# Attention chunks loaded in two row-interleaved transfers, and GpSimd's three products in another order

## The chip, the cores and the metric

The kernel runs on one core of one Trainium2 chip. The metric is the device time of one execution in microseconds, the lower the better. The engines are named as the profile names them: PE is TensorE (PEld its weight loads), DVE is VectorE, ACT is ScalarE, POOL is GpSimd, SP is SyncE, which here only issues DMAs (SPq).

## The reference

Two stages follow one another: a recurrent attention with a decaying state, and a mixture of experts on its output.

```python
B, H, S, D = 4, 8, 768, 48
for t in range(S):                          # per batch and head
    cur   = outer(u * k[t], v[t])
    y[t]  = r[t] @ (state + cur)
    state = w[t][:, None] * state + outer(k[t], v[t])
x = y.transpose(0, 2, 1, 3).reshape(B * S, H * D)     # 3072 tokens of 384
# each token with x @ w_skip > 0 goes to its best of 8 experts:
#   out = x + gate * (relu(x @ w1[e]) @ w2[e]);  other tokens keep x
```

## The kernel before

The attention works on 24 chunks (4 batches times 6 chunks of 128 steps) one after the other. Inside a chunk the recurrence is turned into matrix products. With q the product of the decays from a step to the end of the chunk, and rh the product from its start, the kernel forms three elementwise products, each of 128 x 512 words, all on POOL:

- kq = k times q (line 325 in `prep_keys`), which needs the first scan, q (DVE, line 308 in `prep_scan`);
- rk = r times k (line 317 in `bonus_keys`), which needs only the loaded chunk;
- rp = r times rh (line 334 in `prep_reads`), which needs the second scan, rh (DVE, line 330).

PE multiplies kq with rp into the scores (line 358), DVE masks them (line 364) and multiplies the bonus term (line 381), PE forms the outputs (lines 409 and 413), the state update (line 390), the transposes (line 348), the bonus sums from rk (line 377) and the turned rows (line 425). One pass of the loop over `s` does the outputs of chunk s, the scores of chunk s + 1 and the scans and products of chunk s + 2, so the rp of a chunk is read by PE one pass after it was made. The order of the work on every engine is the order in which it is written, since all of it stands under `tc.manual_schedule()`.

The chunk itself (r, k and w, 1545 words in each row, 128 rows; 96 rows for the two chunks at the ends of the array, which are the chunks 6 and 23 in order of work) is loaded by SP at line 172 into one of three buffers `wrk_sb`. A buffer comes free when the rp of the chunk that was in it is done, so SP waits for POOL before each load. Behind it in SP's queue stand, for each pass, two loads of the turned values vt (line 157), one of v (line 177), the store of an earlier chunk's output (line 435), and in nine passes a part of the expert weights (line 86). Chunks 0 to 4 are loaded in two column parts (`cuts`), the others in one piece. POOL also has the low halves of the weights to form in some passes (line 109) and one-hot rows for the router (line 538).

After the attention comes the mixture of experts, in which PE is busy all the time.

Of the kernel before, what the change touches and what calls it, by code (L numbers as in the profile page):

```python
# [43 lines left out]
V_OFF = K_OFF + NP * P  # L44
# [13 lines left out]
def rwkv_moe_kernel(ctx, tc, wrk, wrk0, vN, uP, wgs, wgp, w12, cst, out):  # L58
    nc = tc.nc
# [82 lines left out]
    with tc.tile_pool(name="att", bufs=2) as att, \  # L142
# [20 lines left out]
        cuts = {i: ((0, R_OFF), (R_OFF, V_OFF)) for i in range(5)}  # L163

        def load_chunk(i):
            b, c = seq[i]
            rows = wrk.rearrange("b c g d n -> (b c g d) n")
            at = 2 * D * chunk[i]
            t = wrk_sb[i % NBUF]
            to, at = (t, at - KO) if 0 < chunk[i] < n - 1 else (t[KO:LO], at)  # L170
            for c0, c1 in cuts.get(i, ((0, V_OFF),)):
                yield nc.sync.dma_start(to[:, c0:c1], rows[at:at + to.shape[0], c0:c1])

        def load_v(i):
            b, c = seq[i]
# [56 lines left out]
        def setup():  # L232
            nc.gpsimd.memset(u_sb, 0.0)
            for t in vt_sb[:3]:
                nc.gpsimd.memset(t, 0.0)
            drain(load_chunk(0))
            second, third = load_chunk(1), load_chunk(2)
            next(second)
            nc.sync.dma_start(c_sb[:, :C_IOTA], cst[:, :C_IOTA])
# [60 lines left out]
        def prep_scan(i):  # L300
            wk = work[i] = {}
            t = wrk_sb[i % NBUF]
            n_ = NP * CW
            a3 = lambda z: z.rearrange("p (a j) -> p a j", a=NP)
            wk["w"] = t
            wk["r"], wk["k"] = a3(t[:, R_OFF:K_OFF]), a3(t[:, K_OFF:V_OFF])
            q = wk["q"] = att.tile([P, NP, CW], F32, tag="q", name=f"q{i}", bufs=2)
            nc.vector.tensor_tensor_scan(  # L308
                q.rearrange("p a j -> p (a j)")[:, ::-1], t[:, 1:1 + n_][:, ::-1],
                ones_at[:, 1:1 + n_][:, ::-1], 0.0, op0=ALU.mult, op1=ALU.max)  # L310
            rk = wk["rk"] = att.tile([P, NP, P], F32, tag="rk", name=f"rk{i}")
            if i > 1:
                bonus_keys(i)

        def bonus_keys(i):
            t = wrk_sb[i % NBUF]
            nc.gpsimd.tensor_tensor(work[i]["rk"].rearrange("p a j -> p (a j)"),  # L317
                                    t[:, R_OFF:K_OFF], t[:, K_OFF:V_OFF], op=ALU.mult)

        def prep_keys(i):  # L320
            wk = work[i]
            heads = wk["w"][:, 0:NP * CW].rearrange("p (a j) -> p a j", a=NP)
            nc.vector.reciprocal(heads[:, :, 0:1], wk["q"][:, :, 0:1])
            kq = wk["kq"] = att.tile([P, NP, P], F32, tag="kq", name=f"kq{i}")
            nc.gpsimd.tensor_tensor(kq, wk["k"], wk["q"][:, :, 1:1 + P], op=ALU.mult)  # L325

        def prep_reads(i):
            wk = work[i]
            rh = wk["rh"] = att.tile([P, NP, CW], F32, tag="rh", name=f"rh{i}", bufs=2)
            nc.vector.tensor_tensor_scan(  # L330
                rh.rearrange("p a j -> p (a j)"), wk["w"][:, 0:NP * CW], reads_at[:, :NP * CW],
                rowsk, op0=ALU.mult, op1=ALU.max)
            rp = wk["rp"] = att.tile([P, NP, P], F32, tag="rp", name=f"rp{i}", bufs=3)
            nc.gpsimd.tensor_tensor(rp, wk["r"], rh[:, :, :P], op=ALU.mult)  # L334
            if i < 2:
                bonus_keys(i)
# [344 lines left out]
        with tc.manual_schedule():  # L681
# [3 lines left out]
            for s in range(-2, n + 1):  # L685
                on = lambda i: 0 <= i < n
                if s == -2:
# [4 lines left out]
                    for g in range(2):  # L692
                        at = 2 * (g ^ 1)
                        nc.sync.dma_start(wgp_sb[half(1), g, :, 2 * D:],
                                          wgp[half(g), at:at + 2, 2 * D:])
                if 3 <= s + 4 < n:
                    chunk_parts = load_chunk(s + 4)
                    if s + 4 in cuts:
                        next(chunk_parts)
                        load_v(s + 2)  # L700
                    drain(chunk_parts)
# [21 lines left out]
                if on(s + 2):  # L723
                    prep_scan(s + 2)
# [3 lines left out]
                if on(s + 2):  # L728
                    prep_keys(s + 2)
                    drip(pace[0])  # L730
                    prep_reads(s + 2)
# [387 lines left out]
```

## Time and profile before

| what | value |
|---|---|
| median of 3 runs | 279.83 us (278.13 to 283.46) |
| the profiled execution, its own time | 279.76 us |
| its span | 277.9 us |
| PE busy | 264.4 us (95%) |
| DVE busy | 211.9 us (76%) |
| ACT busy | 157.1 us (57%) |
| POOL busy | 146.6 us (53%) |
| chunk loads in one piece (128 rows) | 17, 772.5 KB each, 7.1 us from issue to landing in the median |

The shares are means over two unlike stages. The attention takes the first 130 us or so, the experts the rest; the change touches the first alone, so its views are read by stretch.

### The profile page before, as it was taken

The numbers are of one execution on the slowest core, as the hardware profiler recorded it, in microseconds if no ns is written. First come the engines' busy times: TensorE is split into PE (matmuls) and PEld (weight loads), VectorE is DVE, ScalarE is ACT, GpSimd is POOL, SyncE is SP. The second block draws the span as 40 slices with busy tenths as digits, with TensorE's granted clock in tenths as the row PEclk, the third lists the DMA queues.
The fourth block names the chain that finished last, engine by engine and source line by source line (L and its number), as shares of the span: only waits on it lengthen the run. The fifth ranks groups of instructions, "written<-read, shape, count | busy, mean of one in ns | idle before, by whom it ended". The sixth has DMA issues, their size and how long they took to land.

```text
span 277.9 us, 8937 instructions
## 1 busy us (share of the span) xinstructions
PE 264.4 (95%) x3599; PEld 244.0 (88%) x3600; DVE 211.9 (76%) x396; ACT 157.1 (57%) x456; POOL 146.6 (53%) x141
## 2 busy tenths in 40 slices
PE   8899799998999999899999999999999999999992
PEld 3688688887888888787999999999999999999992
DVE  7989789999999999972748597957859488594310
ACT  4365556775788857767326482926729276391300
POOL 6888677798999997984656636011030110201111
PEclk9999999999999999999999999999999999999998
DMA  7999999999877999961078997765662656700001
GB/s 244 279 300 326 322 331 366 374 333 312 270 229 253 319 351 344 267 233 61 28 227 302 337 310 255 240 229 225 225 248 81 235 212 226 266 14 28 9 5 42
DMA packets 26402, 64.33 MB, mean 231 GB/s; under 512 B 4062, under 2 KB 15380, under 8 KB 26352
## 3 DMA queue, kind: packets, MB, share of 16 engines
q1 hardware_dynamic: 24176, 58.37, 63.2%
q0 software_dynamic: 2048, 5.30, 6.0%
q8 instruction: 30, 0.49, 0.7%
q14 instruction: 20, 0.16, 0.2%
q10 hardware_dynamic: 128, 0.00, 0.0%
HBM read 56.61 MB, written 7.67 MB: 231 GB/s over the span
## 4 chain that ended last, share of the span: by engine, by line
PE 71%; DMA 8%; issue 6%; DVE 5%; POOL 4%; ACT 4%; SPq 0%; POOLq 0%; DVEq 0%
PE psO L927 7%; PE psO L929 7%; PE psO L928 6%; PE psH L901 6%; PE psH L902 6%; PE psH L903 6%; PE psY L409 6%; DMA wrk<-wrk 5%; PE psH L135 4%; PE psX L425 4%; PE psA L358 4%; PE psY L413 3%; PE psT L348 3%; PE psY L377 2%; DMA r<-w 2%
## 5 line engine op out<-in xcount | busy, mean ns | idle before, releaser
L838 POOL DMA_INDIRECT out<-fin,ids x16 | 16.9, 1054 | 95.2 <-DVE fin L936 89.2
L908 ACT ACTIVATE hh<-psH 128x240 fp32r<-128x240 f32 (+1 forms) x60 | 22.4, 374 | 54.4 <-PE psH L903 47.4
L901 PE MATMUL psH<-xTh,w1h 128*128 128x240 f32 x168 | 46.3, 276 | 0.0
L902 PE MATMUL psH<-xTl,w1h 128*128 128x240 f32 x168 | 46.3, 276 | 0.0
L903 PE MATMUL psH<-xTh,w1l 128*128 128x240 f32 x168 | 46.1, 274 | 0.0
L927 PE MATMUL psO<-w2h,hh 128*128 128x384 f32 (+1 forms) x120 | 40.9, 341 | 0.0
L929 PE MATMUL psO<-w2h,hl 128*128 128x384 f32 (+1 forms) x120 | 40.3, 335 | 0.0
L928 PE MATMUL psO<-w2l,hh 128*128 128x384 f32 (+1 forms) x120 | 40.2, 335 | 0.0
L364 DVE TENSOR_TENSOR asb<-psA,c_sb 128x512 f32<-128x512 f32 x48 | 30.6, 679 | 5.4 <-PE psA L358 5.3
L913 DVE SCALAR_TENSOR_TENSOR hl<-psH,hh 128x240 fp32r<-128x240 f32 (+1 forms) x60 | 24.2, 403 | 12.3 <-ACT hh L908 7.3
L317 POOL TENSOR_TENSOR rk<-wrk 128x512 f32<-128x512 f32 x24 | 30.7, 1278 | 4.2 <-DMA wrk<-wrk 1.6
L330 DVE TENSOR_TENSOR_SCAN rh<-wrk,rowsk,pss 128x520 f32<-128x520 f32 x24 | 31.1, 1297 | 2.3
L325 POOL TENSOR_TENSOR kq<-wrk,q 128x512 f32<-128x512 f32 x24 | 28.3, 1181 | 6.9 <-DVE q L308 4.9
L901 PEld LDWEIGHTS psH<-xTh,w1h 128*128 128x128 f32 x168 | 31.7, 189 | 0.1
L903 PEld LDWEIGHTS psH<-xTh,w1l 128*128 128x128 f32 x168 | 31.8, 189 | 0.0
L902 PEld LDWEIGHTS psH<-xTl,w1h 128*128 128x128 f32 x168 | 31.7, 189 | 0.0
L334 POOL TENSOR_TENSOR rp<-wrk,rh 128x512 f32<-128x512 f32 x24 | 28.4, 1182 | 5.4 <-DVE rh L330 4.1
L308 DVE TENSOR_TENSOR_SCAN q<-wrk,pss 128x520 f32<-128x520 f32 x24 | 29.5, 1229 | 0.6 <-ACT pss L595 0.4
L409 PE MATMUL psY<-asb,v 128*48 128x128 f32 x384 | 26.9, 275 | 2.6 <-DVE psY L381 2.5
L91 DVE TENSOR_TENSOR w2l<-r,w2h 128x512 fp32r<-128x512 f32 x42 | 27.8, 687 | 1.7 <-ACT w2h L90 1.6
L418 ACT COPY xT<-psY 128x512 f32<-128x512 f32 x24 | 14.1, 588 | 25.6 <-PE psY L413 20.6
L936 DVE SCALAR_TENSOR_TENSOR fin<-psO,gates,xg 128x384 f32<-128x384 f32 (+1 forms) x15 | 9.3, 618 | 25.0 <-PE psO L929 23.2
(159 smaller groups left out, 605.8 us busy)
## 6 DMA issues: line engine op xcount, KB each, us to landing
r<-w SPq DMA_DIRECT2D x48, 512.0 KB, 5.6
wrk<-wrk SPq DMA_DIRECT2D x17, 772.5 KB, 7.1
vt<-wrk SPq DMA_DIRECT2D x48, 96.0 KB, 5.8
v<-vN SPq DMA_DIRECT2D x24, 192.0 KB, 4.9
out<-x SPq DMA_DIRECT2D x24, 192.0 KB, 5.0
wrk<-wrk SPq DMA_DIRECT2D x5, 512.0 KB
wrk<-wrk SPq DMA_DIRECT2D x5, 260.5 KB
wrk<-wrk SPq DMA_DIRECT2D x2, 579.4 KB
```

What stands on the lines that cost most here:

```text
L308: nc.vector.tensor_tensor_scan(q.rearrange("p a j -> p (a j)")[:, ::-1], t[:, 1:1 + n_][:, ::-1], ones_at[:, 1:1 + n_][:, ::-1], 0.0, op0= ...
L317: nc.gpsimd.tensor_tensor(work[i]["rk"].rearrange("p a j -> p (a j)"), t[:, R_OFF:K_OFF], t[:, K_OFF:V_OFF], op=ALU.mult)
L330: nc.vector.tensor_tensor_scan(rh.rearrange("p a j -> p (a j)"), wk["w"][:, 0:NP * CW], reads_at[:, :NP * CW], rowsk, op0=ALU.mult, op1=AL ...
L334: nc.gpsimd.tensor_tensor(rp, wk["r"], rh[:, :, :P], op=ALU.mult)
L364: nc.vector.tensor_tensor(s, psa[g], tri.rearrange("p (o j) -> p o j", o=1).to_broadcast([P, NP, P]), op=ALU.mult)
L409: nc.tensor.matmul(y_at(a, g), v[:, 2 * a + g], wk["asb"][g][:, a], start=False, stop=True, skip_group_check=True)
L901: nc.tensor.matmul(ps, w1h[:, o:o + P], xTh[:, kc], start=(kc == 0), stop=False)
L902: nc.tensor.matmul(ps, w1h[:, o:o + P], xTl[:, kc], start=False, stop=False)
L903: nc.tensor.matmul(ps, w1l[:, o:o + P], xTh[:, kc], start=False, stop=(kc == KC - 1))
L927: nc.tensor.matmul(po, h[j, fc][0], w2h[:, o], start=(fc == 0), stop=False)
L928: nc.tensor.matmul(po, h[j, fc][0], w2l[:, o], start=False, stop=False)
L929: nc.tensor.matmul(po, h[j, fc][1], w2h[:, o], start=False, stop=(fc == FC - 1))
```

## The change

Chunks from 5 on, so far one DMA each, are loaded with two: the even rows and then the odd rows of the same tile, 64 rows each (48 for the two shorter chunks). The call of `bonus_keys` moves from the end of `prep_scan` to the end of `prep_keys`. From chunk 2 on, POOL then forms kq, rk, rp in place of rk, kq, rp.

```diff
-            for c0, c1 in cuts.get(i, ((0, V_OFF),)):
-                yield nc.sync.dma_start(to[:, c0:c1], rows[at:at + to.shape[0], c0:c1])
+            m = to.shape[0]
+            if i in cuts:
+                for c0, c1 in cuts[i]:
+                    yield nc.sync.dma_start(to[:, c0:c1], rows[at:at + m, c0:c1])
+            else:
+                for o in range(2):
+                    yield nc.sync.dma_start(to[o:m:2], rows[at + o:at + m:2, :V_OFF])
...
             rk = wk["rk"] = att.tile([P, NP, P], F32, tag="rk", name=f"rk{i}")
-            if i > 1:
-                bonus_keys(i)
...
             nc.gpsimd.tensor_tensor(kq, wk["k"], wk["q"][:, :, 1:1 + P], op=ALU.mult)
+            if i > 1:
+                bonus_keys(i)
```

On POOL, for chunks 5 and 6, before (the names carry the tile's number in the program; what stands in brackets are the counters that the instruction waits for, the DMAHW ones those of landed DMAs):

```order
L317 TENSOR_TENSOR rk_559<-wrk_90 128x512 [waits DMAHW4_49,PE_49,Pool_49]
L325 TENSOR_TENSOR kq_578<-wrk_90,q_557 128x512 [waits DVE_49,PE_49]
L334 TENSOR_TENSOR rp_582<-wrk_90,rh_580 128x512 [waits DVE_49]
L317 TENSOR_TENSOR rk_654<-wrk_88 128x512 [waits DMAHW2_49,PE_49,Pool_49]
L325 TENSOR_TENSOR kq_673<-wrk_88,q_652 128x512 [waits DVE_49,PE_49]
L334 TENSOR_TENSOR rp_677<-wrk_88,rh_675 128x512 [waits DVE_49]
```

And the same place after (lines 328, 320 and 339 are the old 325, 317 and 334):

```order
L328 TENSOR_TENSOR kq_580<-wrk_90,q_560 128x512 [waits DMAHW4_49,DMAHW5_49,DVE_49,PE_49]
L320 TENSOR_TENSOR rk_562<-wrk_90 128x512 [waits Pool_49]
L339 TENSOR_TENSOR rp_585<-wrk_90,rh_583 128x512 [waits DVE_49]
L328 TENSOR_TENSOR kq_676<-wrk_88,q_656 128x512 [waits DMAHW3_49,DMAHW4_49,DVE_49,PE_49]
L320 TENSOR_TENSOR rk_658<-wrk_88 128x512 [waits Pool_49]
L339 TENSOR_TENSOR rp_681<-wrk_88,rh_679 128x512 [waits DVE_49]
```

The product that needs no scan moved from ahead of the first scan's product to between the two that need scans, and the first product of a chunk waits for two landings.

On SP, from the load of chunk 6 on, before:

```order
L172 DMA wrk_88<-wrk 96x1545 [waits DMAHW2_49,Pool_49]
L157 DMA vt_92<-wrk 48x2x256 [waits DMAHW3_49]
L157 DMA vt_92<-wrk 48x2x256 [waits DMAHW4_49]
L177 DMA v_448<-vN 128x384 [waits DMAHW5_49,PE_49]
L435 DMA out<-x_451 128x384 [waits DMAHW6_49,Activation_49]
L172 DMA wrk_89<-wrk 128x1545 [waits DMAHW7_49,Pool_49]
L157 DMA vt_93<-wrk 48x2x256 [waits DMAHW0_49]
L157 DMA vt_93<-wrk 48x2x256 [waits DMAHW1_49]
L177 DMA v_543<-vN 128x384 [waits DMAHW2_49,PE_49]
```

And after (line 177 is now the chunk load, 182 the load of v, 440 the store):

```order
L177 DMA wrk_88<-wrk 48x1545 [waits DMAHW3_49,Pool_49]
L177 DMA wrk_88<-wrk 48x1545 [waits DMAHW4_49]
L157 DMA vt_92<-wrk 48x2x256 [waits DMAHW5_49]
L157 DMA vt_92<-wrk 48x2x256 [waits DMAHW6_49]
L182 DMA v_450<-vN 128x384 [waits DMAHW7_49,PE_49]
L440 DMA out<-x_453 128x384 [waits DMAHW0_49,Activation_49]
L177 DMA wrk_89<-wrk 64x1545 [waits DMAHW1_49,Pool_49]
L177 DMA wrk_89<-wrk 64x1545 [waits DMAHW2_49]
L157 DMA vt_93<-wrk 48x2x256 [waits DMAHW3_49]
```

Each pass has one DMA more. The eight landing counters are used in turn, so each DMA waits until the eighth one before it has landed: before, that made the load of v wait for the chunk load of the pass before (DMAHW2 above); after, it is the first load of vt that does (DMAHW3).

## Rows read from the trace of the kernel before

**Rows 1.** Busy time over the steady attention: engine busy us, instructions, PEclk, DMA share, GB/s
```profile
core 0: us, PE busy (x) PEld busy (x) DVE busy (x) ACT busy (x) POOL busy (x), PEclk, DMA share, GB/s
20.00:120.00 100.00, 94.95 (x2071) 83.20 (x2070) 93.04 (x144) 69.05 (x240) 87.07 (x81) 1.00 0.98 314
```
**Rows 2.** What PE waited for from 8 to 133 us: total us, times, longest
```profile
PE psY L409 <- DVE psY L381: 2.5, 5, 0.9
PE psY L377 <- issue: 1.6, 1, 1.6
PE psY L377 <- ACT xT L418: 1.1, 2, 0.9
```
**Rows 3.** Timeline of one pass with POOL idle: start us, us, engine, line
```profile
47.77 1.18 POOL L325 TENSOR_TENSOR kq<-wrk,q 128x512 f32<-128x512 f32 x1 [0.56 <-DVE q L308]
47.95 1.30 DVE L330 TENSOR_TENSOR_SCAN rh<-wrk,rowsk,pss 128x520 f32<-128x520 f32 x1
48.22 1.05 PE L358 MATMUL psA<-rp,kq 64*64 64x128 f32 x32
49.32 1.18 POOL L334 TENSOR_TENSOR rp<-wrk,rh 128x512 f32<-128x512 f32 x1 [0.38 <-PE psA L358]
50.46 1.29 POOL L317 TENSOR_TENSOR rk<-wrk 128x512 f32<-128x512 f32 x1
50.53 0.33 SPq L172 DMA_DIRECT2D wrk<-wrk  x1
53.09 1.05 PE L358 MATMUL psA<-rp,kq 64*64 64x128 f32 x32
```
**Rows 4.** Timeline of passes in which POOL is full, chunks 14 and 16
```profile
71.14 1.28 POOL L109 TENSOR_TENSOR w2l<-r,w2h 128x512 fp32r<-128x512 f32 x1
72.13 1.23 DVE L308 TENSOR_TENSOR_SCAN q<-wrk,pss 128x520 f32<-128x520 f32 x1
72.38 1.30 POOL L317 TENSOR_TENSOR rk<-wrk 128x512 f32<-128x512 f32 x1
73.63 1.19 POOL L325 TENSOR_TENSOR kq<-wrk,q 128x512 f32<-128x512 f32 x1
75.05 1.20 POOL L334 TENSOR_TENSOR rp<-wrk,rh 128x512 f32<-128x512 f32 x1
...
86.53 1.19 POOL L334 TENSOR_TENSOR rp<-wrk,rh 128x512 f32<-128x512 f32 x1
...
88.05 1.05 PE L358 MATMUL psA<-rp,kq 64*64 64x128 f32 x32
```
**Rows 5.** What SP's queue waited for: total us, times, longest
```profile
SPq L172 <- POOL rp L334: 21.2, 13, 3.1
...
SPq L157 <- DMA wrk<-wrk: 10.4, 7, 2.4
SPq L177 <- DMA wrk<-wrk: 10.1, 8, 2.0
```
**Rows 6.** The load of chunk 22 (issue, time to landing) and its first scan
```profile
101.00 0.33 SPq L172 DMA_DIRECT2D wrk<-wrk  x1
...
DMA to landing us min/median/max: 8.1/8.1/8.1
...
112.09 1.23 DVE L308 TENSOR_TENSOR_SCAN q<-wrk,pss 128x520 f32<-128x520 f32 x1
```
**Rows 7.** The first scan's own semaphore waits over the run: ns min/median/max
```profile
L308 DVEq EVENT_SEMAPHORE  x23: 21/136/1374, 3.4 to 116.0; - x23
```
**Rows 8.** The last chunk load, of 96 rows, and four stretches as in rows 1
```profile
106.64 0.34 SPq L172 DMA_DIRECT2D wrk<-wrk  x1
...
25.50:29.60 4.10, 3.55 (x95) 2.96 (x94) 3.82 (x6) 2.48 (x11) 3.35 (x3) 1.00 1.06 285
33.70:37.90 4.20, 3.75 (x86) 3.13 (x83) 3.30 (x5) 2.84 (x12) 3.07 (x3) 1.00 1.05 345
43.20:47.40 4.20, 4.20 (x94) 3.76 (x91) 4.09 (x6) 3.26 (x11) 3.60 (x3) 1.00 1.03 364
...
109.50:114.70 5.20, 4.80 (x105) 4.24 (x101) 4.99 (x11) 4.30 (x16) 4.84 (x5) 1.00 1.04 248
```

## The prediction

> **What bounds the kernel now.** [...] Four resources are nearly full, so the shares do not say which ends last. The list of what PE waited for does [rows 2]: in the whole stage it has six entries that sum to 6.3 us, the three largest are shown, and neither POOL nor a transfer is among the six (one of them, the 1.6 us, is a wait for nothing that the profile shows). PE and, close behind it, DVE set the pace. The timeline of a plain pass shows the pace as the distance between the scores of two chunks: 53.09 − 48.22 = 4.87 us [rows 3]. POOL and the transfers run beside this, and what counts of them is their margin.
>
> The margin of rp, the product that PE waits for: in the plain pass rp ends at 49.32 + 1.18 = 50.50 and its chunk's scores start at 53.09, so it has 2.6 us to spare [rows 3]. Where POOL also makes low halves and one-hot rows it runs without a pause and falls behind: the rp of chunk 16 ends at 86.53 + 1.19 = 87.72 and the scores start at 88.05, which leaves 0.33 us [rows 4].
>
> The margin of the chunk loads: SP issues a load as soon as rp frees the buffer (rp ends at 50.50, issue at 50.53 [rows 3]); SP is there first in 13 of them and waits 21.2 us in sum [rows 5]. The slowest load that the trace times is that of chunk 22: issued at 101.00, landed 8.1 us later at 109.1; its scan starts at 112.09, so 3.0 us are left [rows 6].
>
> **The change part by part.**
>
> *Order on POOL.* No product is added. In a plain pass kq starts when the first scan is done, before and after alike; POOL was idle there for 0.56 us, so rk did not hold it up [rows 3]. What changes is rp: it started at 49.32, when the second scan was done (47.95 + 1.30 = 49.25). After the change POOL goes from kq (47.77 + 1.18 = 48.95) to rk for 1.28 us and is free for rp at 50.2, so rp is some 0.8 us late by these rows (0.7 if successive products overlap by 0.05 us, as the starts of rp and rk, 1.14 us apart at 1.18 us each, show). PE's 2.6 us cover it: cost 0. The next load of the buffer is issued 0.8 us later too, and its 3.0 us cover that.
>
> In the full stretch the order would not matter if POOL never paused, but it will pause once: at chunk 14, POOL ended its extra work at 72.4 and did rk while the first scan ran (72.13 + 1.23 = 73.36) [rows 4]. After the change it must wait for that scan, and then does kq and rk (1.19 + 1.30) before rp, which starts at 75.9 instead of 75.05: 0.9 us late. POOL has no pause for the next passes, so the delay stays until it has one. At chunk 16 it meets a margin of 0.33 us, and PE starts the scores 0.9 − 0.33 = 0.55 us late. Once the pass has slipped by this, the later chunks have that much more margin. Cost 0.55 us, once; the bounds are 0 (if the small pauses ahead absorb it) and 0.9 us (if the next chunk has no margin at all).
>
> Does an earlier kq give something back? It can start at most one rk, 1.3 us, earlier in the full stretch. The transposes that read it stand behind the scores on PE, and those wait for rp. Gain 0.
>
> *One more wait.* Chunks 5 to 23 are 19 first scans that wait for two landings instead of one. The semaphore waits in front of this scan took at least 21 ns and 136 ns in the median [rows 7], most of it while DVE was still at work. 19 x 0.021 = 0.4 us is the cost if none is hidden, 0 if all is; a bound from the median is 2.6 us, but that contains true waiting. I take 0.2.
>
> *One more DMA on SP.* Issuing takes 0.33 us [rows 3], 19 times, in a queue that now waits 21 us for rp [rows 5]. Each DMA also waits for the eighth before it. That made the load of v wait for the chunk load of the pass before (10.1 us in 8 waits) [rows 5]; now the first vt load does, one DMA earlier in the queue, and v, the store and the weights stand behind it. They have a pass or more to spare. The next chunk load stands behind them too, but as a rule waits for rp even longer: cost 0.
>
> *Two half loads for one.* The bytes are the same, and so is the size of a row. Nothing can use the even rows alone, since the scan runs over all partitions at once: there is no gain from the first half's landing. The second issue is 0.4 us later than the first, and with rp's 0.8 us this makes 1.2 of the 3.0 us margin. If the halves move as fast as the whole, cost 0. If they do not, the price is in rows of this trace: two loads have 96 rows and not 128, and while they moved the queues were as full as ever, but carried less. The last, issued at 106.64, was under way in the stretch from 109.5 to 114.7: DMA share 1.04, but 248 GB/s; the other, of chunk 6, in that from 25.5 to 29.6: 1.06 and 285 GB/s. Like stretches with 128 rows moved 345 and 364 GB/s [rows 8]. So the way in which rows fall on the DMA engines matters here. In time: 5.2 us x (1 − 248/364) = 1.7 us lost with one load, and 4.1 us x (1 − 285/345) = 0.7 us with the other. No row shows 64 rows at a step of two at this size; the bounds are 0 and 1.7 us of DMA time for each load. I take a value near 0 for the forecast, because the halves are 64 and 64 rows, which 16 engines share as evenly as 128, where a 96-row tile begins at the 17th partition; the rest is the first rival.
>
> [...]
>
> *The sum.* 279.76 us of the profiled execution (277.9 of span and 1.9 around it; 0.07 below the median of the runs) + 0.55 (rp at chunk 16) + 0.2 (semaphores) + 0 (SP) + some 0.4 for a load that comes too late now and then where the weights share the queues = 280.9, so 281.
>
> **The rivals.**
>
> *The halves move slowly, and the DMA engines become the bound: slower.* For it: the rows of the 96-row loads, and that the engines have little room, 98% busy [rows 1]. Against it: what two halves cost is not in the trace. Price: 0.7 to 1.7 us for each of 19 loads, 13 to 32 us of DMA time. Room: the stage moves 31.4 MB in 100 us; at the 350 GB/s of the good stretches that is 90 us, so 10 us are free, and the landing margin gives 2 us more once. Left are 1 to 20 us: 281 to 300, and at the middle price of 1.2 us (23 us in sum) 11 us, 291. It decides from about 0.6 us for a load on (12 us in sum); 0.9 us a load (17 us) make 5 us and so pass 2%.
>
> *Eight landings in flight are too few.* Where the weights also stand in the queue (nine passes), SP's pass is two chunk issues (0.8), a wait of up to 2.4 us for the earlier load [rows 5] and four or five issues of 0.4: about 5.2 us against a pace of 4.87. The next load is then up to 0.35 us later in each of the nine passes, 3.2 us in sum, of which the margin covers 1.8. That gives 281 + 1.4, some 282, and shows as SP arriving after rp.
>
> *It is faster.* The ceiling is all of PE's waits in the stage, 6.3 us: 273.5. For it speaks only that POOL's first product could hold up something that the lists do not name; against it that PE's list does not name POOL at all.
>
> **How the numbers follow.** Forecast as summed, 281: 0.55. Slow halves: 0.33, of which 0.25 lie above 2%. Eight landings: 0.08. Faster: 0.04. Two per cent, 5.6 us, is about what a measurement of this kernel can tell from no change; its bounds are 274.2 and 285.4. Faster: 0.04. Slower: 0.25 from the halves and 0.05 from errors of the other two, 0.30. Within 2%: 0.66. For the range I go down to 278, the lowest run of before, and up to 292, just past the middle price of slow halves; above it lie some 0.12, below it 0.06.
>
> **What the profile after would show.** Right: in plain passes rp starts about 0.8 us later after the second scan, POOL has its pause ahead of kq, the scores still come 4.87 us apart; PE's list has one short wait for rp near 88 us; the chunk loads land with 1.5 us or more ahead of their scans; the stretch from 20 to 120 us moves the same 314 GB/s. Wrong: if DVE's first scan waits for wrk, or the GB/s fall at a DMA share of 1, the halves are slow; if SP issues chunk loads long after rp's end, the eight landings bind; if PE waits for rp in many passes, I have the margin of rp wrong.

## The result, and the profile after

The changed kernel takes 282.38 us (median of 6 runs, 281.13 to 285.49), the kernel before in the same comparison 280.15 us (6 runs, 278.13 to 283.46). The ratio is 1.010, with a 95% interval from 1.0058 to 1.0141: a small loss, of about 2.8 us by this ratio, inside the 2% band. Ratios, here and below, leave out on both sides the executions over 1.5% longer than the fastest of their kernel, so they differ a little from the ratio of the medians (here 1.008), and the traces of the 1 KB DMA and of the four buffers, which are of such executions, are left out. The profiled execution of the changed kernel took 281.13 us with a span of 279.3 us; that of the kernel before took 279.76 and 277.9.

The steady stretch, in the columns of [rows 1]:

```profile
20.00:120.00 100.00, 94.30 (x2037) 82.20 (x2040) 90.67 (x141) 67.71 (x234) 85.10 (x79) 1.00 0.95 306
```

All engines are a little less busy, the clock is the same, and the DMA engines fell from 0.98 to 0.95 and from 314 to 306 GB/s. They did not become full and slow; they stood idle more often.

What PE waited for from 8 to 133 us (total us, times, longest), the counterpart of [rows 2]:

```profile
PE psY L414 <- DVE psY L386: 4.2, 7, 1.7
...
PE psA L363 <- POOL rp L339: 0.6, 1, 0.6
```

PE now waits once for rp, 0.6 us. The other growth is behind DVE. What DVE's first scan waited for:

```profile
DVE q L313 <- DMA wrk<-wrk: 2.6, 2, 1.4
DVE q L313 <- ACT pss L600: 1.5, 1, 1.5
```

A chunk load came too late for the scan twice (at chunk 5 by 1.2 us, at chunk 11 by 1.4), which it did not in the trace of before, and once the scan waited 1.5 us for a copy on ACT (0.4 us before). What SP waited for, beside [rows 5]:

```profile
SPq L177 <- POOL rp L339: 8.8, 5, 2.6
SPq L157 <- DMA wrk<-wrk: 8.1, 12, 1.4
SPq L177 <- DMA wrk<-wrk: 4.2, 7, 0.8
SPq L182 <- DMA wrk<-wrk: 2.5, 3, 1.1
```

L177 is now the chunk load and L182 the load of v. SP was at the chunk load before rp freed the buffer 5 times, not 13, and the chunk load itself waited for landings 7 times. Its waits for landed chunk loads did not grow in sum: 8.1 + 4.2 + 2.5 = 14.8 us, where the two entries of [rows 5] make 20.5. What grew is the time that an issue takes. The issues of the chunk loads from 20 to 120 us, before and after (count, then shortest, median and longest in ns):

```profile
L172 SPq DMA_DIRECT2D wrk<-wrk x18: 327/328/390, 22.1 to 106.6; - x18
```
```profile
L177 SPq DMA_DIRECT2D wrk<-wrk x36: 472/480/1022, 23.3 to 111.6; - x36
```

Two halves take 2 x 0.48 us in the median where one load took 0.33, so 0.63 us more for each chunk and 11 us for the 18. SP's wait for rp shrank by about as much, from 21.2 to 8.8 us.

A plain pass, beside [rows 3]:

```profile
46.73 1.05 PE L363 MATMUL psA<-rp,kq 64*64 64x128 f32 x32
...
51.00 1.18 POOL L328 TENSOR_TENSOR kq<-wrk,q 128x512 f32<-128x512 f32 x1 [1.18 <-DVE q L313]
51.18 1.30 DVE L335 TENSOR_TENSOR_SCAN rh<-wrk,rowsk,pss 128x520 f32<-128x520 f32 x1
...
51.60 1.05 PE L363 MATMUL psA<-rp,kq 64*64 64x128 f32 x32
52.13 1.27 POOL L320 TENSOR_TENSOR rk<-wrk 128x512 f32<-128x512 f32 x1
53.36 1.18 POOL L339 TENSOR_TENSOR rp<-wrk,rh 128x512 f32<-128x512 f32 x1
```

The second scan ends at 51.18 + 1.30 = 52.48 and rp starts at 53.36, 0.88 us later, where it was 0.07 before. The scores come at 51.60 − 46.73 = 4.87 us, as before.

The full stretch, chunks 14 and 16, beside [rows 4]:

```profile
73.66 1.18 POOL L328 TENSOR_TENSOR kq<-wrk,q 128x512 f32<-128x512 f32 x1 [0.26 <-issue]
...
74.79 1.28 POOL L320 TENSOR_TENSOR rk<-wrk 128x512 f32<-128x512 f32 x1
76.03 0.21 POOL L587 TENSOR_TENSOR gds<-gall,vals 128x10 f32<-128x10 f32 x1
76.19 1.19 POOL L339 TENSOR_TENSOR rp<-wrk,rh 128x512 f32<-128x512 f32 x1
...
87.70 1.20 POOL L339 TENSOR_TENSOR rp<-wrk,rh 128x512 f32<-128x512 f32 x1
...
88.95 0.97 PE L363 MATMUL psA<-rp,kq 64*64 64x128 f32 x29 [0.55 <-POOL rp L339]
```

The rp of chunk 16 ends at 88.90 and the scores start at 88.95: the margin of 0.33 us is used up.

The load of chunk 11 (its buffer is freed by the rp in the first row; SP's rows are DMA issues):

```profile
44.10 1.20 POOL L339 TENSOR_TENSOR rp<-wrk,rh 128x512 f32<-128x512 f32 x1
44.21 0.94 SPq L157 DMA_DIRECT2D vt<-wrk  x2
...
45.25 1.09 SPq L182 DMA_DIRECT2D v<-vN  x1
...
46.44 0.38 SPq L440 DMA_DIRECT2D out<-x  x1
46.87 0.42 SPq L86 DMA_DIRECT2D r<-w  x1
...
47.38 1.21 SPq L177 DMA_DIRECT2D wrk<-wrk  x2
...
56.00 1.24 DVE L313 TENSOR_TENSOR_SCAN q<-wrk,pss 128x520 f32<-128x520 f32 x1 [1.40 <-DMA wrk<-wrk]
```

The buffer was free at 45.30, but SP came to the two halves at 47.38, 2.1 us late: it was still getting through the turned rows, v, the store and a weight load. The scan stood still for 1.40 us. In [rows 3] the issue follows the end of rp by 0.03 us. Before, the load of chunk 11 went out 2.22 us ahead of the scores of chunk 8 (48.22 in [rows 3]):

```profile
46.00 0.33 SPq L172 DMA_DIRECT2D wrk<-wrk  x1
```

After, its first half went out 0.65 us behind these scores (46.73), so 2.9 us later against the pace.

The end of the stage, chunk 23:

```profile
118.14 1.20 POOL L339 TENSOR_TENSOR rp<-wrk,rh 128x512 f32<-128x512 f32 x1
119.28 0.23 POOL L591 TENSOR_TENSOR vals<-gds,vals 128x8 bf16<-128x8 f32 x1
119.54 0.20 ACT L600 CAST pss<-vals 128x40 f32<-128x40 bf16 x1 [1.29 <-POOL vals L591]
119.77 1.24 DVE L313 TENSOR_TENSOR_SCAN q<-wrk,pss 128x520 f32<-128x520 f32 x1 [1.50 <-ACT pss L600]
```

A small product of the router (vals) stands behind rp on POOL; ACT copies it, and DVE's last first scan comes behind that copy. So a late rp makes this scan late, whether or not PE needs the rp.

**Where the time went.** The table gives, from the timelines, the start of a chunk's scores minus the start of the same chunk's scores in the kernel before, in us. A step between two columns is time lost there, by whatever cause. The kernels of the other rows are those of the experiments.

| kernel | chunk 9 | 13 | 15 | 16 | 22 | 23 |
|---|---|---|---|---|---|---|
| changed kernel | −1.49 | +0.17 | +0.17 | +0.90 | +0.89 | +1.58 |
| order alone | +1.18 | +1.95 | +1.95 | +2.68 | +2.66 | +3.34 |
| split alone | −1.07 | +1.99 | +1.37 | +1.37 | +1.36 | +1.36 |
| new order where POOL pauses | −1.13 | −1.05 | −1.05 | −0.65 | −0.66 | +0.02 |
| new order for chunks 2 to 13 | −0.26 | +0.12 | +0.13 | +0.52 | +0.51 | +0.50 |
| split with paired v | −1.68 | −1.24 | −1.24 | −1.24 | −1.23 | −1.23 |
| order kq, rp, rk | −1.93 | −0.31 | −0.21 | −0.13 | +0.76 | +1.48 |

The offset at chunk 9 is no part of the change: the profiled execution of before had the 1.6 us wait for nothing that the profile shows [rows 2], which some profiled executions have, of either order (2.1 us in the order alone), and others not. The late scan of chunk 5 lies ahead of chunk 9 as well, so what it cost is hidden in the offset. From there the changed kernel loses 1.66 us by chunk 13 (late loads), 0.73 at chunk 16 (rp) and 0.69 at chunk 23 (the router's product): 3.08 us in one execution, by the ratio 2.8.

### The profile page after: what moved, and what is told of

Same layout as the page of the kernel before. It is cut to its first block, busy times and chain, and to the rows that moved or that the text cites. A ratio compares the mean times of both kernels' runs of the same rounds, so it can differ in the third digit from the quotient of the medians.

```text
span 279.3 us, 8971 instructions
## 1 busy us (share of the span) xinstructions
PE 265.2 (95%) x3599; PEld 244.2 (87%) x3600; DVE 211.4 (76%) x396; ACT 157.4 (56%) x456; POOL 146.9 (53%) x141
## 3 DMA queue, kind: packets, MB, share of 16 engines
q1 hardware_dynamic: 24480, 58.37, 62.7%
## 4 chain that ended last, share of the span: by engine, by line
PE 48%; issue 4%; POOL 3%; ACT 1%; DVE 0%; POOLq 0%
PE psO L932 7%; PE psO L934 6%; PE psO L933 6%; PE psH L907 6%; PE psH L906 6%; PE psH L908 6%; PE psH L135 4%; PE psX L836 2%; PE psO L676 2%; PE psY L414 1%; POOL out L843 1%; POOL hot L543 1%; PE psY L418 1%; POOL rk L320 0%; ACT xT L423 0%
```

## The experiments

All ratios are to the kernel before, run on the same chip. Line numbers differ by a few from kernel to kernel.

### Each part alone

The order alone: rk issued behind kq, chunk loads in one piece.

```
-            if i > 1:
-                bonus_keys(i)          # behind the first scan
...
+            if i > 1:
+                bonus_keys(i)          # behind kq
```

> Only the order on POOL (kq, rk, rp); chunk loads in one piece. If the order costs what the trace after shows (PE waits 0.6 us for rp at chunk 16, and the last scan waits for the router's values that stand behind rp on POOL, 0.7 us more): 0.7 to 1.5 us, ratio 1.003 to 1.006, with one PE wait for rp near 88 us and no scan that waits for wrk. If the late loads were all of the cost: ratio within 0.001 of 1, and no PE wait for rp.

Measured: 280.75 us (12 runs), ratio 1.0059 [1.0017, 1.0101]. PE's and DVE's waits:

```profile
PE psA L358 <- POOL rp L334: 0.5, 1, 0.5
...
DVE q L308 <- ACT pss L595: 1.5, 1, 1.5
```

The same two losses as in the changed kernel, 0.73 at chunk 16 and 0.68 at chunk 23 in the table, and no first scan waits for a load. Together 1.4 us; the ratio is worth 1.6. The table's step of 0.77 us from chunk 9 to 13 is not put down to the order: most of it is a wait of PE of 0.6 us for nothing that the profile shows (line 348), and the kernel with paired v alone, in the old order, has the same wait.

The split alone: two loads of alternate rows from chunk 5 on, the old order.

```
+                for o in range(2):
+                    yield nc.sync.dma_start(to[o:m:2], rows[at + o:at + m:2, :V_OFF])
```

> Only the two row-interleaved loads; old order on POOL. If the eight landing counters are the cause (one DMA more in each pass): 0.5 to 1.7 us, ratio 1.002 to 1.006; SP comes to a chunk load after rp has ended in passes with weights, and one or two scans wait up to 1.5 us for wrk; the stretch 20 to 120 moves 305 to 315 GB/s. If slow rows were the cause: ratio above 1.01 and fewer GB/s at a DMA share of 1. If only the order costs: ratio within 0.001 of 1.

Measured: 280.73 us (12 runs), ratio 1.0064 [1.0028, 1.0100]. DVE's and SP's waits:

```profile
DVE q L313 <- DMA wrk<-wrk: 3.0, 3, 1.6
```
```profile
SPq L157 <- DMA wrk<-wrk: 8.6, 14, 1.3
SPq L177 <- POOL rp L339: 7.8, 5, 2.0
SPq L177 <- DMA wrk<-wrk: 5.4, 8, 1.5
```

PE waits nowhere for rp, the table shows no loss at chunks 16 and 23, and the late loads are there, at chunks 5, 11 and 12. So in these traces the two parts cost separate things, and 0.6% + 0.6% makes about the 1.0% of both, within the intervals.

This execution lost more by the late loads than the changed kernel did (2.44 us against 1.66), and TensorE's clock has a part in it. Behind the late scans of chunks 11 and 12 PE stood still for 2.35 us, and then the granted clock fell to 0.50 for some 3 us (its mean from 20 to 120 us is 0.98):

```profile
66.95 1.08 PE L414 MATMUL psY<-asb,v 128*48 128x128 f32 x16 [2.35 <-DVE psY L386]
...
68.64 1.70 PE L363 MATMUL psA<-rp,kq 64*64 64x128 f32 x29
```
```profile
69.00:70.00 1.00, 1.00 (x30) 1.00 (x27) 0.90 (x3) 0.52 (x1) 1.00 (x1) 0.50 1.07 432
```

The scores, 1.05 us in a plain pass, took over 1.70. The table's +1.99 at chunk 13 holds this; by chunk 15 0.62 us of it had come back, and how much of the 2.44 us is left of it no run isolates. In the trace of the changed kernel the longest such wait is 1.70 us, and the clock stayed at 1.00.

### Is it the way in which the rows fall?

Two halves of neighbouring rows (0 to 63, 64 to 127) in place of even and odd rows; and four interleaved loads of 32 rows. Both with the old order.

```
+                for o in range(2):
+                    ro = slice(o * m // 2, (o + 1) * m // 2)
+                    yield nc.sync.dma_start(to[ro], rows[at + ro.start:at + ro.stop, :V_OFF])
```
```
+                for o in range(4):
+                    yield nc.sync.dma_start(to[o:m:4], rows[at + o:at + m:4, :V_OFF])
```

> Old order on POOL; two loads of neighbouring rows, 0 to 63 and 64 to 127, in place of even and odd. Eight counters: the same as the even and odd rows, ratio 1.002 to 1.006. If it matters which rows one load writes: 64 neighbouring rows move more slowly than 64 at a step of two, the DMA engines are full at 250 to 290 GB/s, scans wait for wrk in many passes, ratio 1.02 to 1.06.

> Old order on POOL; each chunk from 5 on in four interleaved loads of 32 rows. Eight counters: a pass now has eight DMAs, nine with weights, so each waits for its own place in the pass before; a pass cannot be shorter than a load takes to land, 4.5 to 6 us: ratio 1.01 to 1.04, with SP's waits for landed DMAs several times those of two loads. If only the rows and not the number of DMAs mattered: as with two loads.

Measured: neighbouring halves 300.1 us (6 runs), ratio 1.0779 [1.0711, 1.0846]; four loads 289.22 us (6 runs), ratio 1.0409 [1.0339, 1.0480]. The steady stretch, first of the neighbouring halves, then of the four loads:

```profile
20.00:120.00 100.00, 86.94 (x1776) 75.64 (x1775) 80.21 (x121) 58.66 (x200) 74.39 (x66) 0.95 1.04 255
```
```profile
20.00:120.00 100.00, 89.66 (x1901) 78.68 (x1899) 85.78 (x131) 62.78 (x217) 79.03 (x71) 0.98 0.88 280
```

Both move fewer bytes a second, but in opposite ways: with neighbouring halves the DMA engines are full (1.04) at 255 GB/s; with four loads they are less busy (0.88). In both the first scans wait for late loads (7.6 and 5.5 us in sum), and the mean granted clock falls, to 0.95 and 0.98. The page's row of the main DMA queue (packets, MB, share of 16 engines' span) for before, the changed kernel, neighbouring halves and four loads:

```profile
q1 hardware_dynamic: 24176, 58.37, 63.2%
```
```profile
q1 hardware_dynamic: 24480, 58.37, 62.7%
```
```profile
q1 hardware_dynamic: 24480, 58.37, 68.6%
```
```profile
q1 hardware_dynamic: 25056, 58.37, 61.8%
```

Multiplied by the spans (277.9, 279.3, 297.8, 286.5 us) the same 58.37 MB take 175.6, 175.1, 204.3 and 177.1 us of the engines' time. Even and odd rows cost no time on the DMA engines; neighbouring halves cost 28.7 us, or 1.5 us for each of 19 loads. The rival of slow halves is false for this change and true for its neighbour. The four loads cost hardly any engine time either (1.5 us in all), yet 4%: with three more DMAs a pass the engines are not fed. SP's waits and its issues of chunk loads in that kernel:

```profile
SPq L157 <- DMA wrk<-wrk: 1.6, 1, 1.6
SPq L177 <- DMA wrk<-wrk: 1.5, 3, 0.8
```
```profile
L177 SPq DMA_DIRECT2D wrk<-wrk x70: 469/586/1597, 19.6 to 116.0; - x70
```

I had expected several times the waits of two loads (8.6 and 5.4), and they nearly vanish. Four issues of 0.59 us take 2.3 us of a pass of 4.87, and those of the other DMAs come on top. By these rows issuing fills the queue here, and not waits for landings.

Neighbouring halves and alternate rows are the same bytes in the same 24480 packets, and the first took 204.3 us of the engines' time, the second 175.1. What makes the difference no run here shows.

### Is it one DMA more?

The kernel before, with a DMA of 1 KB that nobody reads, behind each chunk load from 5 on; no half loads, old order.

```
+            if i not in cuts:
+                yield nc.sync.dma_start(extra[:, 16 * i:16 * i + 16], cst[:16, 16 * i:16 * i + 16])
```

> Old order, chunk loads in one piece, and behind each from chunk 5 on one DMA of 1 KB that nothing reads: the same number of DMAs in each pass as with two half loads, no row moved otherwise. If the eight landing counters are the cost of the split: as e2, ratio 1.003 to 1.009, with SP waiting for the chunk load of the pass before at the first vt load. If the halves themselves were the cost: ratio within 0.002 of 1.

Measured: 281.31 us (12 runs), ratio 1.0084 [1.0046, 1.0122]. A DMA more in SP's queue costs about as much as the split does, with no chunk load touched. It adds an issue and a landing both, so it does not tell these two apart.

Would a fourth buffer help, so that the loads could be issued a pass earlier? The split alone, with four buffers for the chunks:

```
-        wrk_sb = [pers.tile([P, V_OFF], F32, name=f"wrk{i}") for i in range(NBUF)]
+        NWRK = 4
+        wrk_sb = [pers.tile([P, V_OFF], F32, name=f"wrk{i}") for i in range(NWRK)]
```

> Old order, the two interleaved loads, and four chunk buffers in place of three, so that SP need not wait for the rp of the pass before. If late chunk loads are the cost of the split: they land a pass earlier, no scan waits for wrk, ratio 0.998 to 1.003. If the split costs elsewhere (more semaphores on DVE and POOL): as e2, 1.003 to 1.009.

Measured: 281.67 us (12 runs), ratio 1.0071 [1.0032, 1.0110]. It gives nothing back that can be told from the noise. That fits the waits of the split alone, where SP waits for rp only 5 times (7.8 us): where it comes behind rp anyway, a buffer that is free earlier changes nothing.

And would fewer DMAs? From chunk 6 on one load brings v of two chunks, the same bytes in nine DMAs fewer; once with the split, once without.

```
+            elif i % 2 == 0:
+                v2 = att.tile([P, 2, H, D], F32, tag="v2", name=f"v{i}", bufs=3)
+                nc.sync.dma_start(v2, vN[b, c:c + 2].rearrange("c p h d -> p c h d"))
+                v_sb[i], v_sb[i + 1] = v2[:, 0], v2[:, 1]
```

> The old order on GpSimd, two interleaved half loads as in the change, and from chunk 6 on one load brings v of two chunks: the same bytes, nine DMAs fewer from chunk 7 to 23. If the number of DMAs in flight is what the split costs (one more in each of 19 passes: 1.006), half of them are given back: 1.002 to 1.004 against the kernel before, and SP's waits for landings in the v and turned-row loads fall by about half. If the cost lies in the half loads themselves, it stays at 1.006.

> The kernel before with v of two chunks in one load from chunk 6 on; chunk loads in one piece, old order. If the number of DMAs in flight held anything up before the change, this is faster: 0.996 to 0.999. If the kernel before was never held up there (its first scans wait for no load), 0.998 to 1.002.

Measured: with the split 280.71 us (12 runs), ratio 1.0045 [1.0009, 1.0082]; without 279.56 us (12 runs), ratio 1.0002 [0.9973, 1.0031]. In the first one's trace the split's loss is mostly gone, 0.44 us from chunk 9 to 15 (split alone: 2.44). Its one scan that waits for a load is that of chunk 1, ahead of the split loads:

```profile
7.33 1.24 DVE L318 TENSOR_TENSOR_SCAN q<-wrk,pss 128x520 f32<-128x520 f32 x1 [1.02 <-DMA wrk<-wrk]
```

This execution took 279.23 us, though, 1.5 less than the kernel's median; the median's ratio, 1.0045, lies between the half that was expected and no gain at all, and the interval holds both. Without the split, fewer DMAs change nothing that can be measured.

### The order on GpSimd

The new order only where the trace of before shows pauses on POOL (chunks 2 to 13, 20 and 21); then for chunks 2 to 13 alone. Chunk loads in one piece.

```
-            if i > 1:
+            if i > 1 and i not in between:
                 bonus_keys(i)          # behind the first scan
...
+        between = set(range(2, 14)) | {20, 21}
...
+            if i in between:
+                bonus_keys(i)          # behind kq
```

> Chunk loads in one piece; kq, rk, rp only for the chunks 2 to 13, 20 and 21, where POOL has pauses; the old order for 14 to 19, 22 and 23. If the late rp at chunk 16 and the late router values at chunk 23 are the cost of the order: ratio 0.998 to 1.002, no PE wait for rp. If the plain passes cost something as well (later issue of the loads): 1.003 or more, with scans that wait for wrk.

> One-piece loads; the new order on GpSimd for chunks 2 to 13 only, the old one from 14 on. If the 0.68 us that the last scan waits longer comes from the new order in chunks 20 and 21, which leaves GpSimd later for its last router product, that wait is back at 0.4 us or less, the pass of chunk 23 loses nothing against the kernel before, and PE waits for rp nowhere: 0.996 to 1.002. If the loss at chunk 23 has another source, the scan still waits about 1.5 us.

Measured: 279.8 us (12 runs), ratio 1.0012 [0.9974, 1.0051]; and 281.19 us (12 runs), ratio 1.0035 [0.9994, 1.0076]. Neither is told apart from no change. The traces say more: the loss at chunk 16 is 0.40 and 0.39 us where it was 0.73, and that at chunk 23 is still 0.68 in the first and gone in the second, whose last scan is back to

```profile
DVE q L308 <- ACT pss L599: 0.3, 1, 0.3
```

So the new order in chunks 20 and 21 is what puts the router's product behind, as expected. My expectation that PE would wait for rp nowhere was wrong: it waits 0.2 us at chunk 16 in both (and 0.8 us at chunk 0 in the second, where the order is the old one). It looks as if POOL enters the full stretch later even when only the chunks ahead of it have the new order.

The other sign, scans that wait for a load, is there in both, at chunks 5 and 6 in the first and 6 and 12 in the second:

```profile
DVE q L308 <- DMA wrk<-wrk: 1.3, 2, 0.7
```
```profile
DVE q L308 <- DMA wrk<-wrk: 1.5, 2, 1.3
```

So late loads are not the split's alone. Whether the later rp brings these is open: the order alone has none, and paired v alone, in the old order, has one of 0.5 us.

The changed kernel with the old order for chunks 14 to 19, 22 and 23 (the first rule above):

> The changed kernel with the old order on GpSimd for chunks 14 to 19, 22 and 23, where it has no pause. If the order and the split cost separate things, what is left is the cost of the split: 1.005 to 1.008 against the kernel before. If they cost the same margin twice, it comes lower than either alone, 1.000 to 1.004.

Measured: 280.9 us (12 runs), ratio 1.0045 [1.0011, 1.0080]. The value is just under the range of the first theory and the interval holds both, so it does not decide between separate costs and a shared margin. The scan waits for a load twice (2.2 us), the clock falls as in the split alone (0.98 from 20 to 120 us), and the last scan waits for ACT's copy (1.5 us), since chunks 20 and 21 keep the new order here: more than the cost of the split was left in.

A third order, to see whether an early rp gains: kq, rp, then rk, chunk loads in one piece.

```
-            if i > 1:
-                bonus_keys(i)          # behind the first scan
...
-            if i < 2:
-                bonus_keys(i)
+            bonus_keys(i)              # behind rp
```

> Chunk loads in one piece; on POOL kq, rp, rk for all chunks. If the order kq, rk, rp costs because rp comes late where POOL is full: here rp comes 1.2 us earlier there, PE never waits for rp, and the cost goes: ratio 0.997 to 1.003; the buffer is released by rk, at the old time or up to 0.7 us later, which the loads' margin covers. If it costs because POOL's first product waits for the scan and so loses time at the start of the full stretch: as e1, ratio 1.003 to 1.007.

Measured: 283.67 us (6 runs), ratio 1.0145 [1.0066, 1.0223]: above both ranges that I had expected. PE's list has one wait for rp, at chunk 0, where the order is the old one; from then on there is none, and the loss at chunk 16 is 0.08 us where it was 0.73 (last row of the table): the early rp does what was expected of it. What stands behind it is late instead. (The step from chunk 9 to 13 goes with a wait of 1.2 us for nothing that the profile shows.) Waits of PE and DVE:

```profile
PE psY L374 <- POOL hot L535: 0.8, 1, 0.8
```
```profile
DVE q L308 <- ACT pss L592: 1.6, 1, 1.6
```

The sums that read rk wait once (0.60 us at chunk 22), and the router's product, now behind rk, makes the last scan late (0.72 us at chunk 23). The chunk buffer comes free behind rk and not rp, and SP waits for that 9 times, 16.0 us in sum. But this execution (281.18 us) was 2.5 us faster than the kernel's median, so these waits do not account for the whole; the rest is open.

## Why the prediction was right, and where not

The forecast was 281.0 us, 1.2 more than the kernel before, and the measured loss is 2.8 us by the ratio (median 282.38). The sign and the band came out; of the size less than half was forecast. That the result lies well inside 278 to 292 is owed to the width of that range, which was made for slow halves that did not come. Of the signs named, those for rp came as forecast (0.8 us later, one short wait near 88 us, the pace unchanged); that chunk loads land 1.5 us or more ahead of their scans and that the stretch moves 314 GB/s did not (two late scans, 306). A first scan that waits for wrk was to mean slow halves, and that reading was wrong: it came without them. Term by term:

**rp in plain passes: right.** 0.8 us late was predicted and 0.81 found (0.88 against 0.07), at no cost: the pace stayed at 4.87 us. POOL's pause is now ahead of kq.

**rp at chunk 16: right in mechanism and nearly in size.** The sum had 0.9 − 0.33 = 0.55 us (its parts make 75.85, so 0.80 late and 0.47). rp ended at 88.90, 1.18 later than in [rows 4]; 0.17 of it the whole kernel was late already, which leaves 1.01. A further small product of the router (gds, 0.21 us) stood ahead of the rp of chunk 14, which the estimate had not counted. The margin is not quite 0.33 either, since the scores start 0.05 after rp's end: 1.01 − 0.28 = 0.73, the step in the table.

**The router behind rp: missed, a term put at 0.** The step "once the pass has slipped by this, the later chunks have that much more margin" holds for the scores, but it looked only at PE as a reader of POOL. POOL's next product, vals, feeds a copy on ACT that stands ahead of the last first scan on DVE. 0.69 us, in the changed kernel as in the order alone, and gone when chunks 20 and 21 keep the old order.

**One more DMA on SP: the step that failed.** "The next chunk load stands behind them too, but as a rule waits for rp even longer: cost 0." SP came to the load ahead of rp 5 times instead of 13, for chunk 11 it was 2.1 us late, and the term "some 0.4" for late loads, which no row gave, measured 1.66 us in this execution, some 1.8 (0.0064 x 280) by the ratio of the split alone. The margin of 3.0 us was read at chunk 22, where the second half was to use 1.2 of it; at chunk 11 the first half alone went out 2.9 us later against the pace. Two issues were taken at 0.33 to 0.4 us each and measured 0.48 each, and the 11 us that they add are about what SP's wait for rp lost.

The rival of the eight landings, with a chance of 0.08, came nearest: its price (1.4 more, some 282) and its sign, SP arriving after rp, were those found. Its name says more than the rows do. SP's waits for landed chunk loads fell, from 20.5 to 14.8 us, and in the kernel of four loads they nearly vanish, while the time of issuing grew. That a DMA more is enough is shown by the 1 KB DMA (1.0084); that it acts by the time of issuing is read from the traces. SP still waits for landings in the passes with late loads, and no run changes the number of counters or the length of an issue by itself, so the share of each is open.

**Half loads: right.** Near 0 was taken, and the engines' time is 175.1 us against 175.6. The rival's bounds of 0.7 to 1.7 us a load are met by neighbouring halves (1.5), so its price was sound and only its case was not this one. The rows ahead of the prediction could not tell the two apart. That rows shared evenly by 16 engines move as fast as a whole load was the author's estimate; neighbouring halves are 64 and 64 rows as well and took 28.7 us more. Why the 96-row loads carried less no run shows.

**Semaphores:** the 0.2 us shows in no wait by itself, and no run isolates it.

The sum with the measured sizes is 0.73 + 0.69 + 1.66 = 3.1 us on 279.76, or 282.8. It leaves out what the late scan of chunk 5 cost. The mean granted clock was 1.00 in the profiled execution of the changed kernel and 0.989 to 0.999 in its five other runs, 0.987 in the profiled execution of the split alone; whether the five hold the same fall is not shown.

## What to carry to other kernels

When a load is split, count the DMAs in its queue first: where the issuing queue has little time left in a pass, one DMA more in each, even of 1 KB, can cost as much as the split itself (here 1.0084 against 1.0064), and here a further buffer did not help (1.0071). Take the length of an issue from a load of the same shape (0.48 us here, where the load before took 0.33). When work is moved on an engine that is nearly full, follow everything behind it to its readers, small helper products too; the path that slipped here, by 0.69 us, ran over a copy on a third engine, not over the reader that one looks at first. A margin read from the trace is worth what it is at its narrowest pass, and here a delay lasted until the engine had its next pause: POOL's rp started 1.14 to 1.17 us behind the kernel before at the chunks 14 to 19 and 0.89 at chunk 20, whose kq came after a pause of 0.79 us. A wait list does not say in which pass a wait fell: look it up in the timeline before it is put down to a change, since the first chunks have waits of their own.

## What was not expected of the hardware

The same bytes in rows of the same size cost very different DMA time by which rows stand in one load: 128 rows in one load or 64 + 64 alternate rows some 175 us in all, 64 + 64 neighbouring rows 204 us, at a DMA share of 1.04 and 255 GB/s. The issue on SP goes the other way: 64 alternate rows took 0.47 us at the shortest, 128 rows in one load or 64 neighbouring rows 0.33 us (in the median 0.48, 0.33 and 0.47).
